# First-layer weights read with a step of two columns, second-layer weights two rows a partition

## The chip, the cores and the metric

The kernel runs on one core of one Trainium2 chip. Times are device microseconds of a whole execution. The time before is the median of three runs, 296.78 us (296.77 to 299.02). One execution was taken by the hardware profiler; its own time was 297.07 us, of which the profile shows a span of 295.2 us.

The engines are named as in the profile: PE is TensorE's matmul, PEld its weight load (which overlaps the matmul before it), DVE VectorE, ACT ScalarE, POOL GpSimd, SP SyncE. An engine with a q behind it is that engine's instruction queue.

## What is computed

A strided sparse attention on 8 batches of 8 heads, 576 positions and 64 features, and a two-layer network on its output. Four heads of each batch look at the last 32 positions, the other four at every 32nd position.

```python
scores = scale * np.matmul(q, k.transpose(0, 1, 3, 2))
mask_local = (rel >= 0) & (rel < stride)
mask_strided = (rel >= 0) & (pos[None, :] % stride == pos[:, None] % stride)
...
attn_out = np.matmul(attn, v)
x = attn_out.transpose(0, 2, 1, 3).reshape(B * S, H * D)     # 4608 x 512
h = x @ w_in                                                 # w_in 512 x 2048
r = np.maximum(h, 0.0)
out = (r * r) @ w_out                                        # w_out 2048 x 512
```

## The kernel before

The attention's output is kept transposed in four tiles `xt[0]` to `xt[3]` of 128 features by 4,608 tokens, in bf16. The network runs over nine chunks of 512 tokens. In each chunk the first layer has 16 *groups*, one for each block `ff` of 128 hidden features: four matmuls (`mm1`, L748) over the four chunks `kk` of the 512 features, with 128x128 weights out of `w_in_b` and 512 tokens of `xt[kk]` as the moving operand, summed in one PSUM bank. ACT takes the bank through Relu (L754), DVE squares the result into `g_sb` (L758). The second layer then has 16 groups of four matmuls (`mm2`, L854) with `g_sb` as weights and 512 columns of `w_out_b` as the moving operand; ACT copies the sum out (L858) and SP stores it. The last two chunks do the second layer with seven products instead of eight (L824), in a 4-byte type.

The order of all work is written by hand. `BATCH0` is a list of steps for the first batch's attention, and in it stand the first matmuls of the network: `P0.01` runs `mm1` of kk = 0 for ff = 0 and 1, `P2.012` kk = 2 for ff = 0, 1 and 2, and so on, in the order 0, 2, 1, 3 of kk, as the four `xt` become ready. Between them stand `E1a/6` (unit 1's transposes, L729, and ACT's copy into `xt[1]`, L732) and `O3/2` (unit 3's 16 small matmuls, L674, and DVE's product into `xt[3]`, L676). The number behind a slash is the PSUM bank. `NP` is the number of groups opened in this way; group `NP` takes the first bank of the pool `pt`, the later ones those of `ph` in turn. After `BATCH0` comes a numbered list of groups, and `PLAN` says which attention steps and loads stand ahead of which group.

The weights are loaded by POOL's DMA queue, which also changes their type from 4 bytes to bf16. `w_in_b` is a tile [128, 4, 2048]: partition, kk, column. It is loaded in four pieces (`load_w_in`, L462) while the attention starts: piece 1 is kk = 0 and 2, piece 2 is kk = 1 and 3, each for the first columns; pieces 3 and 4 are all kk for two later ranges of columns. `w_out_b` is [128, 16, 512]; it is loaded in four pieces of four chunks (`load_w_out`, L466), after the scratch data of the first batch that lie in it (q's and k's rows, and bias terms) have been used.

Waits are set by the recording layer: it compares what an instruction reads with what earlier instructions write, and puts a wait for the writer's semaphore on the reader. Each matmul has a weight load as an instruction of its own ahead of it, with waits of its own. PE runs its matmuls in the order of the program.

Of the kernel before, what the change touches and what calls it, by code (L numbers as in the profile page):

```python
# [13 lines left out]


FIRST = (0, 2, 1, 3)
NP = 5
BATCH0 = """
    c0qa c0kv T0qa/6 w1/7 T0kv/4 z w1/7 S0/0,2 W0q0v/4 W0q1v/5 b2.0/0 W0k0v/6 W0k1a/7 b2.1/2 b3.0/4 S2
    c1qv c1kv T1qv/6 T1kv/7 S3.0 b3.1/0 S3.1 b1.0/2 S1.0 b1.1/6 S1.1 H0v D0/4 N2/0 D1/6 E0a/4 N3/2 O2/0  # L20
    P0.01 E1a/6 P0.2/7 P2.012 O3/2 P0.34/0,1 P2.34 P1.01234 P3.0 P3.1 P3.2 P3.3 P3.4
"""
PLAN = """
0: l1q4+5 l1k4+5
# [143 lines left out]
def kernel(  # L168
# [9 lines left out]
    nc = tc.nc  # L178
# [45 lines left out]
    def bank(nm):  # L224
        if places:
            return all_banks[places.pop(0)]
        t = banks[nm].pop(0)
        banks[nm].append(t)
        while id(t) in unread:
            run_due(lambda x: x[1] == unread[id(t)])  # L230
        return t
# [27 lines left out]
    w_in_b = singles.tile([128, 4, d_ff], BF16)  # L259
    w_out_b = singles.tile([128, 16, d_model], BF16)  # L260
# [8 lines left out]
    rv0 = b0[:, n_s:n_s + 8 * S].bitcast(FP32).rearrange("p (u c) -> p u c", u=4)  # L269

    w_in_v = moe_w_in.rearrange("(c p) f -> p c f", p=128)
    w_out_v = moe_w_out.rearrange("(c p) f -> p c f", p=128)

    units = [(b, p) for b in range(B) for p in range(H // 2)]
    st = {}
# [181 lines left out]
            st.setdefault(4 * b + u, {})["v"] = t[:, u]  # L457

    def load_w_in(i):
        f = slice(*((0, 640), (0, 640), (640, 1344), (1344, 2048))[i])  # L460
        c = (slice(0, 4, 2), slice(1, 4, 2), slice(0, 4), slice(0, 4))[i]
        nc.gpsimd.dma_start(out=w_in_b[:, c, f], in_=w_in_v[:, c, f])  # L462

    def load_w_out(i):
        c = slice(4 * i, 4 * (i + 1))
        nc.gpsimd.dma_start(out=w_out_b[:, c, :], in_=w_out_v[:, c, :])  # L466

    clock = [0]
    pending = []
# [1 line left out]
    def later(n, fn, key=None):  # L471
        pending.append((clock[0] + n, key, fn))
# [267 lines left out]
    def mm1(c, ff, kks=range(4), order=range(4), pool=None):  # L740
        if c not in gs:
            gs[c] = g_pool.tile([128, 16, 512], BF16, name="g_sb")
        g = gs[c]
        if kks[0] == order[0]:
            phs[ff] = bank(pool or "ph")
        ph = phs[ff]
        for kk in kks:
            nc.tensor.matmul(ph, w_in_b[:, kk, 128 * ff:128 * (ff + 1)],  # L748
                             xt[kk][:, 512 * c:512 * (c + 1)],
                             start=(kk == order[0]), stop=(kk == order[-1]))  # L750
        if kks[-1] != order[-1]:
            return
        r = r_pool.tile([128, 512], BF16, name="r")
        nc.scalar.activation(r, ph, AF.Relu)  # L754
        if c in SEVEN:
            later(1, lambda: squares(c, ff, r))
            return
        later(1, lambda: nc.vector.tensor_tensor(g[:, ff, :], r, r, op=ALU.mult))  # L758
# [22 lines left out]
    def squares(c, ff, r):  # L781
        g, i = gs[c], ff % 8
        if not ss:
            att.close()
            late = ctx.enter_context(tc.tile_pool(name="sums", bufs=1, reuse_waits="tile"))
            for nm in ("1", "2", "3", "4", "a"):
                ss[nm] = late.tile([128, 8, 2, 128], mybir.dt.float32r, name=f"s{nm}")
        nc.vector.tensor_tensor(g[:, ff, :], r, r, op=ALU.mult)  # L788
        if ff < 8:
            return  # L790
        S = {k: x[:, i] for k, x in ss.items()}
        a1, a2 = (g[:, k, :].rearrange("p (u t c) -> p u t c", u=2, t=2) for k in (i, ff))
        nc.gpsimd.tensor_copy(S["a"], a2[:, :, 1])  # L793
        nc.vector.tensor_tensor(S["1"], a1[:, :, 1], a2[:, :, 1], op=ALU.add)
        nc.vector.tensor_tensor(S["2"], S["1"], a1[:, :, 0], op=ALU.subtract)
        last = lambda: nc.vector.tensor_tensor(S["4"], a2[:, :, 0], S["2"], op=ALU.subtract)
        later(15 + (4, 4, 5, 6, 7, 8, 9, 10)[i] - 2 * i, last)
        if i < 7:
            return
        for k in range(0, 8, 4):  # L800
            a1 = g[:, k:k + 4, :].rearrange("p k (u t c) -> p (k u) t c", u=2, t=2)
            nc.vector.tensor_tensor(ss["3"][:, k:k + 4].rearrange("p k u c -> p (k u) c"), a1[:, :, 0], a1[:, :, 1],
                                    op=ALU.subtract)
# [71 lines left out]
    def first_part(kks, ffs):  # L875
        for ff in ffs:
            mm1(0, ff, kks, FIRST, None if ff < 2 else "py")

    def run_step(word):
# [40 lines left out]
        elif op == "C":  # L920
            load_str_tall(int(arg[:-1]), arg[-1])
        elif op == "Q":
            load_qk_rows(int(arg[:-1]), arg[-1])
        elif op == "X":
            transpose_str(int(arg[:-1]), arg[-1])
        elif op == "A":
            transpose_cast(int(arg[:-1]), arg[-1])
        elif op == "R":
            order_local(int(arg[:-2]), arg[-2], ENG[arg[-1]])
        elif op == "Y":  # L930
            transpose_local(int(arg))
        elif op == "V":
            (load_v_local_sw if int(arg) > 2 else load_v_local_all)(int(arg))
        elif op == "U":
            load_v_str(int(arg))
        elif op == "B":
            spread_v_str(int(arg[0]), int(arg[1]), ENG[arg[2]])
        elif op == "l":
            load_qk_local_sw(int(arg[0]), [int(x) for x in arg[2:].split("+")], arg[1])
        elif op == "r":  # L940
            load_str_rows(int(arg[0]), arg[1])
        elif op == "i":
            load_w_in(int(arg))
        elif op == "o":
            load_w_out(int(arg))
        elif op == "z":
            late_constants()
        else:
            raise ValueError(word)
# [64 lines left out]
    for i in range(4):  # L1014
        load_w_in(i)
# [8 lines left out]
    def add(c, kind, i, pool=None):  # L1024
        if kind == 0:
            groups.append(lambda: None)
        elif kind == 1:
            groups.append(lambda: mm1(c, i, pool=pool))
        elif c in SEVEN:
            groups.append(lambda: mm2_7(c, i) if i < 14 else None)  # L1030
        else:
            groups.append(lambda: mm2(c, i, pool))

    for ff in range(16):
        add(0, 1, ff, {NP: "pt", 8: "py"}.get(ff)) if ff >= NP else add(0, 0, ff)
    for part in range(4):
# [58 lines left out]
```

## Time and profile before

| | |
|---|---|
| median of three runs | 296.78 us |
| the profiled execution | 297.07 us |
| its span | 295.2 us |
| matmuls of the first layer (L748), in the records | 557, 131.7 us busy |
| matmuls of the second layer (L854), in the records | 432, 100.9 us busy |
| first and last start of a first-layer matmul | 17.2 and 278.2 us |
| issue of w_in's four pieces by POOL | from 7.6 to 9.8 us |
| issue of w_out's four pieces by POOL | 15.3 to 32.6 us |

Lines of a timeline give the start, the duration from the first start to the last end, the engine, the line, the operation and the count; in brackets stands the idle time before it and what ended it. A matmul's duration in the records is modelled and longer than the distance to the next one, since matmuls are pipelined; the distance between starts is what counts. Some records of matmuls are missing. In rows of one line of code, durations stand as smallest, median and largest.

### The profile page before, as it was taken

The numbers are of one execution on the slowest core, as the hardware profiler recorded it, in microseconds if no ns is written. First come the engines' busy times: TensorE is split into PE (matmuls) and PEld (weight loads), VectorE is DVE, ScalarE is ACT, GpSimd is POOL, SyncE is SP. The second block draws the span as 40 slices with busy tenths as digits, with TensorE's granted clock in tenths as the row PEclk, the third lists the DMA queues.
The fourth block names the chain that finished last, engine by engine and source line by source line (L and its number), as shares of the span: only waits on it lengthen the run. The fifth ranks groups of instructions, "written<-read, shape, count | busy, mean of one in ns | idle before, by whom it ended". The sixth has DMA issues, their size and how long they took to land.

```text
span 295.2 us, 5895 instructions
## 1 busy us (share of the span) xinstructions
PE 286.3 (97%) x2177; PEld 155.7 (53%) x2212; DVE 210.5 (71%) x553; ACT 170.7 (58%) x321; POOL 83.0 (28%) x123
## 2 busy tenths in 40 slices
PE   7899999999999999999999999999999999999995
PEld 3554555545545454554454445544454444894594
DVE  6557687697666759678367835675489969968983
ACT  3758846775668736774577447645665466307610
POOL 8874743004513008119303800000000013102300
PEclk9999999999999999999999999999999999999999
DMA  7999999999999999999999999411011110021003
GB/s 149 188 207 204 192 198 190 150 204 215 147 138 213 117 163 201 136 166 141 216 159 147 165 186 147 83 56 73 36 23 52 58 54 0 1 104 42 0 2 142
DMA packets 91724, 37.38 MB, mean 127 GB/s; under 512 B 77548, under 2 KB 85830, under 8 KB 91696
## 3 DMA queue, kind: packets, MB, share of 16 engines
q0 software_dynamic: 50608, 18.33, 57.2%
q1 hardware_dynamic: 40944, 18.62, 34.3%
q8 instruction: 17, 0.28, 0.4%
q14 instruction: 11, 0.09, 0.1%
q10 hardware_dynamic: 144, 0.07, 0.1%
HBM read 37.22 MB, written 9.44 MB: 158 GB/s over the span
## 4 chain that ended last, share of the span: by engine, by line
PE 94%; DMA 2%; issue 1%; DVE 1%; ACT 0%; POOL 0%; DVEq 0%; POOLq 0%
PE psb L748 42%; PE psb L854 33%; PE psb L824 9%; DMA w_out_b<-in_k_dram 2%; PE psb L707 2%; PE psb L625 1%; PE psb L611 1%; PE psb L622 1%; PE psb L587 1%; PE psb L542 1%; PE psb L490 1%; PE psb L729 0%; PE psb L512 0%; PE psb L337 0%; DVE x_l L696 0%
## 5 line engine op out<-in xcount | busy, mean ns | idle before, releaser
L748 PE MATMUL psb<-xt,w_in_b 128*128 128x512 bf16 x557 | 131.7, 379 | 1.1
L754 ACT ACTIVATE r<-psb 128x512 bf16<-128x512 f32 x144 | 85.4, 599 | 47.2 <-PE psb L748 41.8
L854 PE MATMUL psb<-w_out_b,g_sb 128*128 128x512 bf16 x432 | 100.9, 379 | 1.1 <-issue 0.5
L748 PEld LDWEIGHTS <-w_in_b 128*128 128x128 bf16 x576 | 53.2, 97 | 58.3 <-issue 0.9
L758 DVE TENSOR_TENSOR g_sb<-r 128x512 bf16<-128x512 bf16 x112 | 47.1, 423 | 37.0 <-ACT r L754 36.1
L854 PEld LDWEIGHTS <-g_sb 128*128 128x128 bf16 x448 | 41.0, 97 | 44.7
L793 POOL CAST sa<-g_sb 128x256 fp32r<-128x256 bf16 x16 | 9.7, 607 | 100.3 <-DVE g_sb L788 100.3
L638 DVE TENSOR_TENSOR xt<-psb,rv 64x144 bf16<-64x144 f32 x84 | 26.2, 311 | 11.5 <-ACT rv L630 10.4
L858 ACT COPY y<-psb 128x512 f32<-128x512 f32 x28 | 16.6, 592 | 29.4 <-PE psb L854 28.4
L628 ACT ACTIVATE rv<-psb 128x432 f32<-128x432 f32 (+1 forms) x21 | 10.5, 501 | 12.8 <-PE psb L622 12.8
L713 DVE TENSOR_TENSOR x_l<-psb,rinv 96x384 bf16<-96x384 f32 x28 | 15.5, 553 | 1.0
L365 POOL DMA_DIRECT2D q_t<-in_q_dram x6 | 3.4, 569 | 45.3 <-DMA qT_s<-q_t 44.0
L788 DVE TENSOR_TENSOR g_sb<-r 128x512 bf16<-128x512 bf16 x32 | 13.0, 420 | 3.7 <-ACT r L754 3.7
L598 ACT ACTIVATE e<-psb 128x384 bf16<-128x384 f32 x30 | 12.0, 510 | 4.2 <-PE psb L587 4.2
L594 DVE TENSOR_TENSOR e<-e,mask_all 128x576 bf16<-128x576 bf16 x20 | 8.4, 456 | 7.3 <-ACT e L598 7.2
L294 POOL DMA_DIRECT2D k_l<-in_k_dram x16 | 12.2, 765 | 3.6 <-DMA v_st<-in_v_dram 3.6
L612 ACT ACTIVATE e<-psb 128x432 bf16<-128x432 f32 (+1 forms) x21 | 10.4, 496 | 4.0 <-PE psb L611 4.0
L645 DVE TENSOR_TENSOR xt<-psb,rv 64x270 bf16<-64x270 f32 (+1 forms) x28 | 9.8, 425 | 3.7 <-ACT rv L630 3.5
L824 PE MATMUL psb<-t,s 128*128 128x256 f32 x96 | 12.2, 283 | 0.0
L294 POOL DMA_DIRECT2D q_l<-in_q_dram x16 | 11.6, 728 | 0.7 <-DMA k_l<-in_k_dram 0.7
L824 PEld LDWEIGHTS psb<-t,s 128*128 128x128 f32 x96 | 11.6, 189 | 0.0
L630 ACT ACTIVATE rv<-rv 128x432 f32<-128x432 f32 (+1 forms) x21 | 11.2, 532 | 0.7
(135 smaller groups left out, 311.0 us busy)
## 6 DMA issues: line engine op xcount, KB each, us to landing
out_dram<-y SPq DMA_DIRECT2D x35, 256.0 KB, 3.8
w_out_b<-in_moe_w_out_dram POOLq DMA_DIRECT2D x4, 512.0 KB, 15.3
q_t<-in_q_dram POOLq DMA_DIRECT2D x7, 288.0 KB, 7.2
k_t<-in_k_dram POOLq DMA_DIRECT2D x7, 288.0 KB, 6.8
vl<-in_v_dram POOLq DMA_DIRECT2D x6, 288.0 KB, 7.3
v_st<-in_v_dram POOLq DMA_DIRECT2D x7, 216.0 KB, 7.8
w_in_b<-in_moe_w_in_dram POOLq DMA_DIRECT2D x2, 704.0 KB, 13.8
k_l<-in_k_dram POOLq DMA_DIRECT2D x16, 72.0 KB, 7.8
```

The lines of the kernel that those rows point to most:

```text
L294: nc.gpsimd.dma_start(out=t[:, :, hh, :], in_=src[b, 2 * p + hh].rearrange("(t p) d -> p t d", p=QL))
L598: nc.scalar.activation(e[:, row, 4 * QL * i:4 * QL * (i + 1)], bk[row][i][:, 0:4 * QL], AF.Exp, scale=scale)
L630: nc.scalar.activation(rv, rv, AF.Exp, scale=-1.0)
L638: nc.vector.tensor_tensor(to[:, :, NJ * part:NJ * (part + 1), par], of, by, op=ALU.mult)
L713: nc.vector.tensor_tensor(x, po[0:QL, :, 0:D], rinv[0:QL].to_broadcast([QL, NL, D]), op=ALU.mult)
L748: nc.tensor.matmul(ph, w_in_b[:, kk, 128 * ff:128 * (ff + 1)], xt[kk][:, 512 * c:512 * (c + 1)], start=(kk == order[0]), stop=(kk == order ...
L754: nc.scalar.activation(r, ph, AF.Relu)
L758: later(1, lambda: nc.vector.tensor_tensor(g[:, ff, :], r, r, op=ALU.mult))
L788: nc.vector.tensor_tensor(g[:, ff, :], r, r, op=ALU.mult)
L824: nc.tensor.matmul(pa, a, b, start=k == 0 and n not in "273", stop=k == 7, skip_group_check=True)
L854: nc.tensor.matmul(py, g[:, ff, 128 * j:128 * (j + 1)], w_out_b[:, ff, :], start=(ff == 0), stop=(ff == 15))
L858: nc.scalar.copy(y, py)
```

## The change

`w_out`'s rows are laid two to a partition: chunks 2m and 2m + 1 of `w_out_b` hold, on partition p, the rows 256m + 2p and 256m + 2p + 1, so a DMA's run in memory is two rows long. The hidden features of two neighbouring groups are interleaved to fit: group ff takes every second column out of the 256 columns of its pair. The first two pieces of `w_in` hold 512 columns instead of 640, the other two 768 instead of 704. Four groups instead of five are opened in `BATCH0`.

```diff
-NP = 5
+NP = 4
 BATCH0 = """
 ...
-    P0.01 E1a/6 P0.2/7 P2.012 O3/2 P0.34/0,1 P2.34 P1.01234 P3.0 P3.1 P3.2 P3.3 P3.4
+    P0.01 E1a/6 P0.2/7 P2.012 O3/2 P0.3/0 P2.3 P1.0123 P3.0 P3.1 P3.2 P3.3
 """
...
-    w_out_v = moe_w_out.rearrange("(c p) f -> p c f", p=128)
+    w_out_v = moe_w_out.rearrange("(m p c) f -> p m (c f)", p=128, c=2)
...
     def load_w_in(i):
-        f = slice(*((0, 640), (0, 640), (640, 1344), (1344, 2048))[i])
+        f = slice(*((0, 512), (0, 512), (512, 1280), (1280, 2048))[i])
         c = (slice(0, 4, 2), slice(1, 4, 2), slice(0, 4), slice(0, 4))[i]
         nc.gpsimd.dma_start(out=w_in_b[:, c, f], in_=w_in_v[:, c, f])

     def load_w_out(i):
         c = slice(4 * i, 4 * (i + 1))
-        nc.gpsimd.dma_start(out=w_out_b[:, c, :], in_=w_out_v[:, c, :])
+        nc.gpsimd.dma_start(out=w_out_b[:, c, :].rearrange("p (m c) f -> p m (c f)", c=2),
+                            in_=w_out_v[:, 2 * i:2 * i + 2])
...
         for kk in kks:
-            nc.tensor.matmul(ph, w_in_b[:, kk, 128 * ff:128 * (ff + 1)],
+            nc.tensor.matmul(ph, w_in_b[:, kk, 256 * (ff // 2):256 * (ff // 2 + 1)].rearrange("p (f c) -> p c f", c=2)[:, ff % 2],
                              xt[kk][:, 512 * c:512 * (c + 1)],
                              start=(kk == order[0]), stop=(kk == order[-1]))
```

## The prediction

> **What bounds the kernel now.** I read the page first: busy shares, then the chain that ended last.
>
> ```profile
> span 295.2 us, 5895 instructions
> PE 286.3 (97%) x2177; PEld 155.7 (53%) x2212; DVE 210.5 (71%) x553; ACT 170.7 (58%) x321; POOL 83.0 (28%) x123
> PE 94%; DMA 2%; issue 1%; DVE 1%; ACT 0%; POOL 0%; DVEq 0%; POOLq 0%
> ```
>
> PE is the bound: 286.3 of 295.2 us busy, and 94% of the chain. An edit can therefore gain only where PE waits, and loses wherever it makes PE wait. The view of waits for PE over the first 60 us says what it waits for, and the windows say how little of that is left later:
>
> ```profile
> engine line waited for: us in total, times, longest us
> PE psb L871 <- DVE xt L980: 1.3, 1, 1.3
> PE psb L347 <- DMA w_out_b<-in_k_dram: 0.8, 1, 0.8
> PE psb L729 <- DVE x_l L696: 0.5, 1, 0.5
> PE psb L542 <- DVE kTl L497: 0.4, 1, 0.4
> ```
> ```profile
> 18.10:25.00 6.90, 6.85 (x46) 3.14 (x46) 3.26 (x7) 4.25 (x9) 3.03 (x4) 1.00 1.21 208
> 34.00:200.00 166.00, 164.39 (x1259) 82.96 (x1281) 115.22 (x319) 103.08 (x199) 47.77 (x66) 1.00 1.31 161
> ```
>
> (Columns: length, then busy time of PE, PEld, DVE, ACT, POOL, the clock, the DMA share, GB/s.) No wait for a load of w_in or of w_out by moe_w_out is on the list; the one w_out_b row is k's rows, parked in that tile. From 18.10 to 25.00 PE is busy 6.85 of 6.90 us: there is no slack in which a new wait could hide.
>
> **A new wait: all of w_in before the second chunk of it.** In the built program's order of PE's instructions, three waits have moved. Before, the weight loads wait for piece 1 at P0's first matmul, piece 2 at P1's first, piece 3 at the sixth group's, piece 4 at the eleventh's. After, P0's first still waits for piece 1 alone, but the first weight load of P2 (kk = 2, ff = 0) waits for pieces 2, 3 and 4 together. The data need none of it: P2 reads chunk 2, columns 0 to 511, which is in piece 1. My reading is that a weight slice with a step of two is compared with the written blocks by its first and last element, so that chunk 2 counts as overlapped by each piece that begins in an earlier chunk and ends in a later one; chunk 0's first columns lie ahead of the others. When is PE there, and when does the last piece land?
>
> ```profile
> 17.58 0.42 PE L729 MATMUL psb<-ident,x_l 96*128 96x96 bf16 x6
> 17.84 1.03 PE L748 MATMUL psb<-xt,w_in_b 128*128 128x512 bf16 x4
> 18.80 0.45 PE L674 MATMUL psb<-e,g_sb 72*64 72x72 bf16 x16
> 19.18 9.24 PE L748 MATMUL psb<-xt,w_in_b 128*128 128x512 bf16 x41
> ```
> ```profile
> L462 POOL DMA_DIRECT2D w_in_b<-in_moe_w_in_dram x4: 738/742/785, 7.6 to 9.8; - x4
> DMA to landing us min/median/max: 8.8/11.0/15.2
> ```
> ```profile
> 25.27 0.54 POOL L427 DMA_DIRECT2D v_st<-in_v_dram  x1 [2.57 <-DMA w_in_b<-in_moe_w_in_dram]
> ```
> ```profile
> 2.76 6.77 DMA w_out_b<-in_k_dram
> 9.52 0.05 issue
> 9.57 0.70 PE psb L347 x12
> ```
>
> The row at 17.84 is P0.2 and P2's three matmuls. A matmul of 512 columns is shown with 0.379 us but they follow each other by (1.03 - 0.38) / 3 = 0.217 us, so PE comes to P2 at 17.84 + 0.22 = 18.06. The last piece is issued at 9.8 and the longest landing is 15.2 us: 25.0, which POOL's row confirms (its v_st load, free to go at 22.70, was held by a w_in landing until 25.27). From a landing to the matmul that waited for it the chain shows 0.05 us (9.52 to 9.57). PE would go on at 25.05: **7.0 us** of idle. Behind the waiting load in PE's order stand P2, unit 3's 16 small matmuls (L674) and all later work; DVE's xt of unit 3, ACT's and DVE's evictions wait for those. Nothing of this can move up, since matmuls run in program order.
>
> The loads themselves hardly move that landing: the four pieces hold the same 4.19 MB as before, on the same queue, behind the same loads, with 1,536 pieces of row in both versions (rows of 2 KB and 3 KB instead of 2.5 and 2.75). Pieces 2 to 4 land within 25.0 - 16.4 = 8.6 us; I take 0 and keep 0.5 us either way. POOL, the issuing engine, isn't held by the wait: what it issues next waits for landings and for PE work that lies before P2; the first of its loads that waits for later PE work is
>
> ```profile
> 36.60 0.54 POOL L365 DMA_DIRECT2D q_t<-in_q_dram  x1 [1.34 <-PE psb L542]
> ```
>
> and moves with PE.
>
> **The clock after that idle time.** Only the start of this kernel shows PE after a long rest.
>
> ```profile
> 1.26 4.02 PE L871 MATMUL psb<-xt 128*128 128x512 bf16 x9 [1.26 <-DVE xt L980]
> 5.53 0.38 PE L871 MATMUL psb<-xt 128*128 128x512 bf16 x1
> L871 PE MATMUL psb<-xt x11: 381/634/634, 1.3 to 6.0; 128*128 128x512 bf16 x11
> ```
>
> The same 128x512 matmul takes 634 ns there and 381 ns from 5.53 on, and the first nine follow each other by (4.02 - 0.63) / 8 = 0.42 us instead of 0.217: half rate for 5.53 - 1.26 = 4.3 us. Half of that, **2.1 us**, is lost if 7.0 us of idle put PE back to that state. No row of before shows an idle time between 1.3 us and that, so the bounds are 0 and, if the slow stretch is half as long again, 3.2 us; I take 2.1, from the only row in which PE starts from rest. The Trainium skill ("TensorE: Matmul & The Clock Gate", section "HAM oscillation — how this bites in real kernels") says that an idle gap of more than about 3.4 us throttles the clock again; by it the 7.0 us are enough and the sum is the one below, without it 2.1 us less; the rule speaks against this change, and no row of before can test it.
>
> **The weight loads with a step of two.** 576 of them.
>
> ```profile
> L748 PEld LDWEIGHTS <-w_in_b 128*128 128x128 bf16 x576 | 53.2, 97 | 58.3 <-issue 0.9
> L824 PEld LDWEIGHTS psb<-t,s 128*128 128x128 f32 x96 | 11.6, 189 | 0.0
> 278.40 3.82 PE L824 MATMUL psb<-w_out_b,g_sb 128*128 128x256 bf16 x32
> 281.98 4.03 PE L824 MATMUL psb<-t,s 128*128 128x256 f32 x32
> 285.85 2.06 PE L824 MATMUL psb<-t,sa 128*128 128x256 f32 x16
> 38.67 0.20 PE psb L611 x8
> ```
>
> No bf16 load of before has a step; the nearest row is the load of 4-byte elements, whose reads are as far apart: 189 ns against 97. Even so it lies under matmuls that last 217 ns, and the 32 such matmuls from 281.98 to 285.85 come every 121 ns, against 112 in the bf16 rows before: so a load can be followed by the next within 121 ns. Inside a run of L748 that is hidden. It would show only where a run begins behind short matmuls (L611: 0.20 / 8 = 25 ns each); by the program's order that is 44 places, such as
>
> ```profile
> 219.11 0.34 PE L707 MATMUL psb<-vl,e 128*128 128x65 bf16 x6
> 219.29 3.62 PE L748 MATMUL psb<-xt,w_in_b 128*128 128x512 bf16 x15
> ```
>
> so at most 44 x (121 - 25) ns = 4.2 us, and 0 if the step costs nothing. A gain is excluded: the reads are no shorter. I take 0, since the type and the count of elements are those of the 97 ns row, and keep 4.2. By the Trainium skill (same page, section "Weight-path perf modes — Fast Weight Load (FWL) and DoubleRow") the fast load holds for 128 weights that aren't fp32 at any column step from -1,023 to 1,024 elements; by that rule the term is 0, by the 189 ns row up to 4.2; no load here has a step, so the trace doesn't say.
>
> **Four groups instead of five.** The fifth group's four matmuls (0.87 us) move from the first part to just behind it: same work on PE. What it thins is a cover. DVE's xt of unit 3 is needed by P3:
>
> ```profile
> 19.36 0.76 DVE L676 TENSOR_TENSOR xt<-psb,g_sb 128x576 bf16<-128x576 f32 x1 [1.44 <-PE psb L674]
> 21.55 4.05 ACT L754 ACTIVATE r<-psb 128x512 bf16<-128x512 f32 x8 [2.65 <-PE psb L748]
> ```
>
> DVE's row ends at 20.12, 1.32 us after L674 began (18.80). Nine matmuls lay between, now six: 0.38 + 6 x 0.217 = 1.68 us, still more than 1.32. Without that cover it would cost up to 0.94 us; at half rate it only grows. Group 5 takes the first bank of the other pool, empty since unit 1's copy; ACT needs 4.05 / 8 = 0.5 us per eviction against 0.87 us per group. Cost 0.
>
> **w_out in rows of two.** Half as many, longer rows. PE waits for none of these loads now, and after a stall of PE they have 9 us more: 0.
>
> **Sum.** The profiled execution took 297.07 us (span 295.2 and 1.87 around it): + 7.0 + 2.1 + 0 + 0 = 306.2. It lies 0.29 above the median of 296.78, so **305.9 us**.
>
> **The rivals.**
> - *The idle time doesn't slow the clock.* For it: PEclk is full in all 40 slices of the page, the start too, so that row can't show it; against it the 634 ns. 305.9 - 2.1 = 303.8. Chance 0.08.
> - *Stall and slow clock, and the stepped loads show at the 44 places.* For it: the 189 ns; against: two bytes each, as before. 305.9 to 310.1; at 121 ns each, 310.1. Chance 0.10.
> - *Not slower: the new wait finds its pieces landed.* If w_in's four pieces went fast enough that the fourth is there when PE comes to P2, PE doesn't stop, the clock stays, and the time is 296.8. The point is 18.06 us; by 21 the loss would fall under 1%. The first piece is there by 7.6 + 8.8 = 16.4, so three pieces would have to follow within 1.7 us instead of 8.6. Against it stand all rows of landings. Chance 0.03, for a mistake of mine in what the wait covers.
>
> **How the numbers follow.** The likeliest case has what is left, 0.79; its own range is 304.6 to 307.5 (landing 0.5 us either way, slow stretch by 1.1 either way, not both in full). The range 303.8 to 308.0 adds the first rival and the lower half of the second; left out are the third and the rest of the second, 0.03 + 0.05, and some 0.1 for a slow stretch or a landing beyond the bounds. 1%, 3.0 us, is about what a measurement of this kernel tells from no change (its runs go from 296.77 to 299.02). All cases but the third lie above that: slower 0.95, within 1% 0.04 (the third, and a landing some microseconds earlier), faster 0.01.
>
> **What would show it.** PE idle for about 7 us from 18 us on, ended by the landing of w_in_b; in the page's slices PE falls in the third and fourth. The first L748 matmuls behind it at over 600 ns, for some 4 us. PEld of L748 tells of the step: 97 ns as before, or near 189, and the starts of L748 behind L707 and L611 whether it shows. ACT's first evictions move from 21.55 to about 30. I am wrong if PE runs on at 18.06, if it goes on much before 25, if its first matmuls last 380 ns, or if L748's runs cost more than 217 ns a matmul.

## The result, and the profile after

The changed kernel takes 306.06 us (median of four runs, 304.91 to 307.35) against 296.77 us before. The ratio of the means of all runs is 1.030, with a 95% interval of 1.023 to 1.036. The forecast was 305.9. The profiled execution is the shortest of the four, 304.91 us with a span of 303.1 us; it is 7.8 us above the profiled execution of before, and 1.2 us below its own median, which matters below.

The two pages first, before and after: PE busy and the clock in 40 slices (7.4 and 7.6 us long), then, of the changed kernel, the chain by engine and by line.

```profile
PE   7899999999999999999999999999999999999995
PEclk9999999999999999999999999999999999999999
```
```profile
span 303.1 us, 5931 instructions
PE   8927999999999999999999999999999999999995
PEclk9986999999999999999999999999999999999999
PE 91%; DMA 4%; POOL 2%; issue 2%; DVE 0%; DVEq 0%; POOLq 0%
PE psb L749 42%; PE psb L855 32%; PE psb L825 9%; DMA w_in_b<-in_moe_w_in_dram 4%; PE psb L708 2%; PE psb L626 1%; PE psb L612 1%; PE psb L623 1%; PE psb L588 1%; PE psb L491 1%; PE psb L543 1%; POOL w_in_b L462 0%; POOL xt L306 0%; POOL vl L440 0%; PE psb L337 0%
```

Before, PE is at 9 tenths in every slice from the third to the last but one. Now the third is at 2 and the fourth at 7, and the clock falls to 8 and 6 tenths in the same two. DMA's share of the chain has risen from 2 to 4%, and the loads on it are new: w_in's, where before's chain has k's rows.

The timeline of PE around that place (start, first start to last end, engine, line, operation, count):

```profile
17.11 0.42 PE L730 MATMUL psb<-ident,x_l 96*128 96x96 bf16 x6
17.37 0.38 PE L749 MATMUL psb<-xt,w_in_b 128*128 128x512 bf16 x1
24.30 1.44 PE L749 MATMUL psb<-xt,w_in_b 128*128 128x512 bf16 x3 [6.55 <-issue]
25.67 0.69 PE L675 MATMUL psb<-e,g_sb 72*64 72x72 bf16 x16
26.29 9.97 PE L749 MATMUL psb<-xt,w_in_b 128*128 128x512 bf16 x42
```

P0.2 runs alone at 17.37. P2's three matmuls, which followed it at once before, start at 24.30. PE would have come to them at 17.37 + 0.22 = 17.59, so the stop costs 6.7 us. That it is a wait although the view says "issue" is seen from who waited for w_in's loads, and from the event that PE's weight-load queue held (L749 is the changed kernel's mm1):

```profile
who waited for it (us, times):
  PEld L749: 6.8, 1
  PE psb L749: 6.6, 1
  POOL v_st L427: 2.8, 1
...
DMA to landing us min/median/max: 8.0/10.0/14.6
```
```profile
L749 PE MATMUL psb<-xt,w_in_b x576: 376/379/634, 16.7 to 286.0; 128*128 128x512 bf16 x192
L749 PEldq EVENT_SEMAPHORE  x2: 51/3764/7477, 16.8 to 121.1; - x2
```

The queue began to wait at 16.8 and was released 7.48 us later, at 24.28. The last piece was issued at 9.6 and landed 14.6 us later, at 24.2. The matmuls behind it last up to 634 ns, the value that only the start of the kernel showed before. The windows (length, busy time of PE, PEld, DVE, ACT, POOL, clock, DMA share, GB/s) show when:

```profile
17.60:20.90 3.30, 0.15 (x1) 0.00 (x0) 0.00 (x0) 0.82 (x2) 2.22 (x3) 1.00 1.16 209
20.90:24.30 3.40, 0.00 (x0) 0.03 (x1) 0.00 (x0) 0.00 (x0) 0.70 (x1) 0.50 1.20 205
24.30:27.70 3.40, 3.40 (x23) 1.38 (x24) 0.76 (x1) 0.00 (x0) 1.95 (x6) 0.50 1.23 212
27.70:34.00 6.30, 6.30 (x31) 2.80 (x29) 3.41 (x8) 4.53 (x9) 5.19 (x8) 1.00 1.56 190
```

The clock is full for 3.3 us of the stop, then half until 27.7. PE works 3.4 us of that, and loses half, 1.7 us. The sum is 6.7 + 1.7 = 8.4; PE reached this place 0.5 us earlier than in the execution of before (P0.2 at 17.37 instead of 17.84), and 8.4 - 0.5 = 7.9 is the difference of the two spans.

Behind it nothing is lost. From the first second-layer matmul to the end of the last row of PE, before and after:

```profile
33.87 0.38 PE L854 MATMUL psb<-w_out_b,g_sb 128*128 128x512 bf16 x1
...
289.63 2.06 PE L824 MATMUL psb<-tb,s 128*128 128x256 f32 x16
```
```profile
41.72 1.03 PE L855 MATMUL psb<-w_out_b,g_sb 128*128 128x512 bf16 x4
...
297.46 2.05 PE L825 MATMUL psb<-tb,s 128*128 128x256 f32 x16
```

291.69 - 33.87 = 257.82 us before, 299.51 - 41.72 = 257.79 after. Most of the 576 first-layer weight loads lie in that stretch, all with a step of two.

### The profile page after: what moved, and what is told of

Its sections match the earlier page's. It is cut to its first block, busy times and chain, and to the rows that moved or that the text cites. A ratio compares the mean times of both kernels' runs of the same rounds, so it can differ in the third digit from the quotient of the medians.

```text
span 303.1 us, 5931 instructions
## 1 busy us (share of the span) xinstructions
PE 290.9 (96%) x2212; PEld 156.6 (52%) x2212; DVE 211.4 (70%) x553; ACT 170.9 (56%) x321; POOL 81.9 (27%) x123
## 4 chain that ended last, share of the span: by engine, by line
PE 91%; DMA 4%; POOL 2%; issue 2%; DVE 0%; DVEq 0%; POOLq 0%
PE psb L749 42%; PE psb L855 32%; PE psb L825 9%; DMA w_in_b<-in_moe_w_in_dram 4%; PE psb L708 2%; PE psb L626 1%; PE psb L612 1%; PE psb L623 1%; PE psb L588 1%; PE psb L491 1%; PE psb L543 1%; POOL w_in_b L462 0%; POOL xt L306 0%; POOL vl L440 0%; PE psb L337 0%
## 5 line engine op out<-in xcount | busy, mean ns | idle before, releaser
L749 PE MATMUL psb<-xt,w_in_b 128*128 128x512 bf16 x576 | 134.7, 381 | 6.7 <-issue 6.6
L755 ACT ACTIVATE r<-psb 128x512 bf16<-128x512 f32 x144 | 85.5, 598 | 55.3 <-PE psb L749 51.4
L855 PE MATMUL psb<-w_out_b,g_sb 128*128 128x512 bf16 x448 | 103.2, 379 | 0.0
L749 PEld LDWEIGHTS <-w_in_b 128*128 128x128 bf16 x576 | 53.5, 98 | 65.7 <-issue 9.0
L639 DVE TENSOR_TENSOR xt<-psb,rv 64x144 bf16<-64x144 f32 x84 | 26.2, 312 | 11.5 <-ACT rv L631 10.4
L825 PEld LDWEIGHTS psb<-t,s 128*128 128x128 f32 x96 | 11.6, 188 | 0.0
```

Of the source, the lines that this page charges most:

```text
L639: nc.vector.tensor_tensor(to[:, :, NJ * part:NJ * (part + 1), par], of, by, op=ALU.mult)
L749: nc.tensor.matmul(ph, w_in_b[:, kk, 256 * (ff // 2):256 * (ff // 2 + 1)].rearrange("p (f c) -> p c f", c=2)[:, ff % 2], xt[kk][:, 512 * c ...
L825: nc.tensor.matmul(pa, a, b, start=k == 0 and n not in "273", stop=k == 7, skip_group_check=True)
L855: nc.tensor.matmul(py, g[:, ff, 128 * j:128 * (j + 1)], w_out_b[:, ff, :], start=(ff == 0), stop=(ff == 15))
```

## The experiments

The theory: PE waits for w_in's last piece because a stepped read is compared with the loads by its first and last element, and after that rest it runs at half clock for some microseconds; step, rows and groups cost nothing by themselves. The rivals: the stepped weight loads cost time; the groups, the pieces or w_out's rows do. `mm1` has another line number in some of the variants (L748 to L755); its tile in the rows shows it.

**Each piece in a tile of its own** (`e1_own_tiles`).

```diff
-    w_in_b = singles.tile([128, 4, d_ff], BF16)
+    w_in_p = [singles.tile([128, n, w], BF16, name=f"w_in{i}") for i, (n, w) in enumerate(((2, 512), (2, 512), (4, 768), (4, 768)))]
...
-        nc.gpsimd.dma_start(out=w_in_b[:, c, f], in_=w_in_v[:, c, f])
+        nc.gpsimd.dma_start(out=w_in_p[i], in_=w_in_v[:, c, f])
+
+    def w_in_of(kk, m):
+        if m < 2:
+            return w_in_p[kk % 2][:, kk // 2, 256 * m:256 * m + 256]
+        return w_in_p[2 + m // 5][:, kk, 256 * ((m - 2) % 3):256 * ((m - 2) % 3) + 256]
...
```

> The changed kernel with each of w_in's four pieces in a tile of its own; the step of two, w_out's rows and the four opened groups stay. P2 then waits for piece 1 alone, which it has. If the joint wait and the clock behind it are all of the loss (my theory), PE runs on at 18 us, no matmul of the first layer after the start takes 634 ns, and the time is 296.8 within 0.6 us. If the stepped weight loads cost something, PE still doesn't stop at 18 us, but the time stays above: up to 301 us if each of the 44 places behind short matmuls shows 96 ns.

297.33 us (median of 12 runs) against 297.16 for the kernel before in the same runs: ratio 1.001, 0.997 to 1.005. PE runs on:

```profile
17.56 1.03 PE L754 MATMUL psb<-xt,w_in 128*128 128x512 bf16 x4
18.52 0.45 PE L680 MATMUL psb<-e,g_sb 72*64 72x72 bf16 x16
18.90 2.33 PE L754 MATMUL psb<-xt,w_in 128*128 128x512 bf16 x10
21.48 7.08 PE L754 MATMUL psb<-xt,w_in 128*128 128x512 bf16 x32 [0.26 <-DMA w_in<-in_moe_w_in_dram]
```

The whole loss is gone with the wait, and the step, the rows and the four groups are all still there. The last row holds something that my prediction didn't have: with four groups opened, the fifth needs piece 3 four matmuls earlier, and in this execution PE waited 0.26 us for it. The ten matmuls ahead of it take 2.33 us, 9 x 0.217 + 0.38, so P3 doesn't wait for unit 3's xt.

**No step** (`e4_no_step`): weights read as before, w_out's rows and their loads as before (those lines are left out here), the rest as changed.

```diff
...
-            nc.tensor.matmul(ph, w_in_b[:, kk, 256 * (ff // 2):256 * (ff // 2 + 1)].rearrange("p (f c) -> p c f", c=2)[:, ff % 2],
+            nc.tensor.matmul(ph, w_in_b[:, kk, 128 * ff:128 * (ff + 1)],
...
```

> The changed kernel with weights read without a step and w_out's rows laid as before; the pieces of 512 and 768 columns and the four opened groups stay. If the step is what brings the joint wait, P2 waits for piece 1 alone and the time is 296.8 within 0.6 us. If the pieces' sizes or the four groups cost anything, it is above that: up to 0.9 us for xt of unit 3 coming late, or the wait for piece 3 at the fifth group, which is now needed 0.9 us earlier.

297.23 us against 297.16, ratio 1.002 (0.999 to 1.004). P2's matmuls follow P0.2 in one row:

```profile
17.82 1.03 PE L748 MATMUL psb<-xt,w_in_b 128*128 128x512 bf16 x4
```

PE has no wait for w_in; its weight load has one of 0.4 us, which is not among PE's waits. Without the step the joint wait is gone (w_out's rows, put back with it, are tested by themselves next); pieces and groups are worth nothing that these runs can tell.

**w_out's rows alone** (`e5_w_out_alone`): the kernel before with these lines of the change. It leaves out the regrouping of w_in's columns to match, so it computes another output, with the same loads and the same work.

```diff
-    w_out_v = moe_w_out.rearrange("(c p) f -> p c f", p=128)
+    w_out_v = moe_w_out.rearrange("(m p c) f -> p m (c f)", p=128, c=2)
...
-        nc.gpsimd.dma_start(out=w_out_b[:, c, :], in_=w_out_v[:, c, :])
+        nc.gpsimd.dma_start(out=w_out_b[:, c, :].rearrange("p (m c) f -> p m (c f)", c=2),
+                            in_=w_out_v[:, 2 * i:2 * i + 2])
```

> The kernel before with w_out loaded in rows of two a partition and nothing else changed; w_in's columns are not regrouped to match, so hidden features meet the wrong rows of w_out and the output differs from the reference's. My theory: PE waits for none of these loads, so 296.8 within 0.6 us, although the loads have half the rows. If w_out's rows matter for PE in some way that the wait list doesn't show, the time leaves that band on either side.

297.23 us against 297.07, ratio 1.001 (0.998 to 1.004).

**The same tile, laid out by piece** (`e6_by_piece`): tests how the wait is found. One tile as in the changed kernel, but the pieces lie one behind the other in it, and piece 1's two chunks are neighbours.

```diff
-    w_in_b = singles.tile([128, 4, d_ff], BF16)
+    w_in_b = singles.tile([128, 4 * d_ff], BF16)
...
-        nc.gpsimd.dma_start(out=w_in_b[:, c, f], in_=w_in_v[:, c, f])
+        o, n = ((0, 2), (1024, 2), (2048, 4), (5120, 4))[i]
+        t = w_in_b[:, o:o + n * (f.stop - f.start)].rearrange("p (c f) -> p c f", c=n)
+        nc.gpsimd.dma_start(out=t, in_=w_in_v[:, c, f])
...
```

> The changed kernel with one tile for w_in as in it, but laid out inside in the order of the pieces (piece 1, 2, 3, 4 one behind the other), so that no piece's first and last element enclose another's. Steps, w_out and groups stay. If a stepped read is compared by its first and last element, P2 waits for piece 1 alone and the time is 297 within 0.6 us, as with four tiles. If any stepped read of a tile waits for all of the tile's loads, P2 stops as in the changed kernel: 306.

297.26 us against 297.07, ratio 1.001 (0.997 to 1.005); P2 follows P0.2 at once:

```profile
17.93 1.03 PE L755 MATMUL psb<-xt,w_in_b 128*128 128x512 bf16 x4
```

So neither one tile nor the step by itself brings the wait: it takes the step together with pieces that lie between one another's first and last element. The runs show which reads wait; how the recording layer compares them is inferred from that. (Its profiled execution took 300.1 us, with one wait of 1.8 us for a transposing load at 90 us that the median doesn't have.)

**Only the last piece apart** (`e2_last_apart`): a shorter stop.

```diff
-    w_in_b = singles.tile([128, 4, d_ff], BF16)
+    w_in_b = singles.tile([128, 4, 1280], BF16)
+    w_in_c = singles.tile([128, 4, 768], BF16, name="w_in_c")
...
-        nc.gpsimd.dma_start(out=w_in_b[:, c, f], in_=w_in_v[:, c, f])
+        nc.gpsimd.dma_start(out=w_in_c if i == 3 else w_in_b[:, c, f], in_=w_in_v[:, c, f])
...
```

> The changed kernel with only piece 4 of w_in in a tile of its own. P2 waits for pieces 2 and 3. The landing theory: PE stops from 17.6 until piece 3 has landed (20.4 in the changed kernel's trace), 2.9 us, which is less than the 3.1 us of rest after which the clock fell there; the clock stays full, so 296.8 + 2.9 = 299.7 us. If the clock falls for any stop of this kind, 1.7 us or more on top, 301.4. If the loss comes from the weight loads and not from the wait's length, about 306 as in the changed kernel.

303.69 us (median), four runs from 301.82 to 303.80; ratio 1.020 (1.017 to 1.024). That is above the 299.7 and the 301.4 that I had set down. The profiled one is that of 301.82:

```profile
17.42 0.38 PE L753 MATMUL psb<-xt,w_in_b 128*128 128x512 bf16 x1
20.52 1.14 PE L753 MATMUL psb<-xt,w_in_b 128*128 128x512 bf16 x3 [2.71 <-DMA w_in_b<-in_moe_w_in_dram]
```
```profile
17.60:20.50 2.90, 0.20 (x1) 0.00 (x0) 0.00 (x0) 0.88 (x2) 2.55 (x3) 1.00 1.15 208
20.50:20.90 0.40, 0.38 (x2) 0.21 (x3) 0.00 (x0) 0.00 (x0) 0.00 (x0) 0.97 1.22 223
20.90:24.30 3.40, 3.40 (x24) 1.28 (x22) 0.76 (x1) 0.00 (x0) 0.70 (x1) 0.50 1.20 205
24.30:34.00 9.70, 9.70 (x56) 4.66 (x55) 6.03 (x15) 7.48 (x14) 6.56 (x12) 1.00 1.43 198
```

The stop is 2.9 us as expected and ends with piece 3, so its length is set by the landing. My expectation for the clock was wrong: it fell, and it fell 0.4 us after PE had gone on, at 20.9. It then stayed at half for 3.4 us of full work: 2.9 + 1.7 = 4.6, against 301.82 - 297.16 = 4.7. The other three runs are 1.9 us longer, and no trace of them was kept. A second slow stretch of that length would cost 1.7. The mean granted clock is on record for each run: 0.994 for the profiled one, which is its 3.4 us at half clock, and 0.989 and 0.987 for two of the others, which is about 7 to 8 us and fits a second stretch. The third has 0.994 too, at 303.80 us, so its extra time stays open.

**A stop filled with work** (`e3_busy_wait`): the wait stays, PE doesn't rest.

```diff
-    P0.01 E1a/6 P0.2/7 P2.012 O3/2 P0.3/0 P2.3 P1.0123 P3.0 P3.1 P3.2 P3.3
+    P0.01 E1a/6 P0.2/7 w31/1 P2.012 O3/2 P0.3/0 P2.3 P1.0123 P3.0 P3.1 P3.2 P3.3
```

> The changed kernel with 31 matmuls of 128x512 on a tile of zeros, whose sums nothing reads, put between P0.2 and P2; they fill the stop (31 x 0.217 = 6.7 us). The joint wait stays. If the clock behind the stop is part of the loss, it stays full now and the time falls by 1.7 us or more against the changed kernel, to 303.3 to 304.4 us, with the first matmuls of P2 at 379 ns. If the loss behind the stop has another cause (evictions, banks, the weight loads), the time stays at 306.

304.32 us (median), four runs from 303.85 to 304.71; ratio 1.024 (1.021 to 1.027).

```profile
17.88 6.85 PE L872 MATMUL psb<-xt 128*128 128x512 bf16 x31
24.74 0.81 PE L749 MATMUL psb<-xt,w_in_b 128*128 128x512 bf16 x3
```
```profile
24.70:34.00 9.30, 9.29 (x58) 4.26 (x58) 4.65 (x10) 5.37 (x10) 6.84 (x12) 1.00 1.44 198
```

P2's three matmuls now take 0.81 us instead of 1.44, the clock is full, and 1.7 us of the loss is gone (2.1 when each kernel is set against the kernel before of its own runs: 9.3 and 7.2 us), while PE comes to P2 later than in the changed kernel's trace (24.74 against 24.30). The clock is a part of the loss of its own. The mean granted clock of every run bears that out: 0.981 or 0.989 in all five executions of the changed kernel, 0.997 or more in all four with the stop filled, and 0.998 or more in 38 of the 42 of the kernel before that ran beside the experiments e1 to e7.

**The changed kernel once more** (`after_again`), for the spread of its times.

> The changed kernel once more, for its clock. In its first trace the clock was halved from 20.9 to 27.7, of which PE worked 3.4 us, and that execution was the shortest of four (304.91 against 305.78 to 307.35). If the slow stretch behind the stop differs from execution to execution, this one's time minus 304.91 is half of its slow working stretch minus 1.7, within 0.5 us. If something else spreads the times, the slow stretch is 3.4 us again whatever the time.

305.39 us, 0.48 above the first trace. The clock:

```profile
21.60:24.40 2.80, 0.00 (x0) 0.00 (x0) 0.00 (x0) 0.00 (x0) 0.27 (x1) 0.51 1.22 205
24.40:28.50 4.10, 4.05 (x24) 1.56 (x25) 0.76 (x1) 0.00 (x0) 2.28 (x7) 0.50 1.22 208
28.50:34.00 5.50, 5.45 (x26) 2.47 (x26) 3.04 (x8) 4.24 (x8) 4.58 (x5) 1.00 1.59 189
```

PE worked 4.05 us at half clock, which makes 2.0 - 1.7 = 0.3 us more than in the first trace; the rest is a stop that begins and ends 0.1 us later. The slow working stretch does differ from execution to execution.

**Larger steps** (`e8_step4`, `e9_step8`, `e7_step16`): the stepped loads by themselves. Each regroups w_in's columns and w_out's rows to match, here for 16:

```diff
-            nc.tensor.matmul(ph, w_in_b[:, kk, 256 * (ff // 2):256 * (ff // 2 + 1)].rearrange("p (f c) -> p c f", c=2)[:, ff % 2],
+            nc.tensor.matmul(ph, w_in_b[:, kk].rearrange("p (f c) -> p c f", c=16)[:, ff],
...
```

> The changed kernel with a step of 16 columns instead of two and w_out's rows 16 a partition. Each group now needs all columns, so already P0 has to wait for pieces 3 and 4: PE stops 0.9 us of work earlier than in the changed kernel, and at the same stretches of slow clock the time is 0.9 us above it, 307.0. If the weight loads slow with the step, the starts behind short matmuls spread (25 and 29 ns in the trace of before) and up to 4.2 us come on top, 311.

> The changed kernel with a step of four columns and w_out's rows four a partition, to see from which step the weight load slows: 98 ns at a step of two, 146 at 16, where some first-layer matmuls come later than 216 ns. If the load grows evenly with the step, about 105 ns here; if there is a threshold, 98. P2's joint wait stays, so PE stops until 24 to 25 us as in the changed kernel, and the time is within 2 us of 306.

> The same with a step of eight and w_out's rows eight a partition. P0 now needs piece 3 (20.4 us), and the group that opens the second half piece 4. Even growth: about 119 ns a load, and less than half of the 1.2 us that the step of 16 lost from its first second-layer matmul to the last of all. A threshold between eight and 16: 98 ns and none of that loss (257.5 us for that stretch).

308.74 us (median of four runs) for 16, which is neither the 307.0 nor the 311 that I had set down; 306.37 and 304.37 (one run each) for four and eight. These times hold stops and slow stretches of differing length, so the loads are read from their own rows; steps 2, 4, 8 and 16, one fence each (busy us, mean ns):

```profile
L749 PEld LDWEIGHTS <-w_in_b 128*128 128x128 bf16 x576 | 53.5, 98 | 65.7 <-issue 9.0
```
```profile
L748 PEld LDWEIGHTS <-w_in_b 128*128 128x128 bf16 x576 | 62.0, 114 | 59.1 <-issue 10.1
```
```profile
L748 PEld LDWEIGHTS <-w_in_b 128*128 128x128 bf16 x576 | 79.2, 146 | 41.8 <-DMA w_in_b<-in_moe_w_in_dram 4.8 <-issue 1.7
```
```profile
L748 PEld LDWEIGHTS <-w_in_b 128*128 128x128 bf16 x576 | 79.4, 146 | 42.8 <-issue 7.5
```

98, 114, 146 and 146 ns: neither of the two courses that I had set down, even growth or a threshold. The stretch from the first second-layer matmul to PE's last row is 257.8 us at a step of two, 258.0 at four, and 259.0 at eight and 16. The last of these from its rows, 303.03 - 44.01:

```profile
44.01 1.03 PE L854 MATMUL psb<-w_out_b,g_sb 128*128 128x512 bf16 x4
...
300.98 2.05 PE L824 MATMUL psb<-tb,s 128*128 128x256 f32 x16
```

So a large step does cost this kernel something, 1.2 us, but a step of two costs nothing. The stretch tells such differences: in the traces with a step of two of the changed kernel, once more, e1, e2 and e3 it goes from 257.79 to 257.81 us.

## Why the prediction was right

- **The new wait.** Forecast 7.0 us of stop from 18.06 to 25.05; measured 6.7, from 17.6 to 24.3. The place, what is waited for and the release by the fourth piece are as forecast. Both ends came earlier in this execution. The explanation by first and last element, an inference then, is borne out by the one tile laid out by piece. One reading beside it was wrong: the first of POOL's loads put down to PE work behind P2 isn't that at 36.60 but w_out's second, at 21.94 (first line). In the changed kernel it goes at 20.96 (second line), while PE stands still, so it didn't hang on that work and POOL wasn't held, as forecast. ACT's first eviction came at 28.7, not at about 30: with four groups, three matmuls fewer lie ahead of it, which the sign left out.

```profile
21.94 0.76 POOL L466 DMA_DIRECT2D w_out_b<-in_moe_w_out_dram  x1 [1.27 <-PE psb L748]
20.96 0.70 POOL L466 DMA_DIRECT2D w_out_b<-in_moe_w_out_dram  x1 [0.85 <-DMA w_in_b<-in_moe_w_in_dram]
```

- **The clock.** Forecast 2.1 us from the kernel's start, where PE runs at half rate for 4.3 us. Measured 1.7 and 2.0 us in two traces of the changed kernel; filling the stop takes 1.7 to 2.1 off the median. The Trainium skill's rule that speaks against the change ("TensorE: Matmul & The Clock Gate", "HAM oscillation — how this bites in real kernels": an idle gap of more than about 3.4 us throttles the clock) agrees with these traces, though a gap of 2.9 us did so too. That the clock would be halved behind the stop was right; that the size came near is partly luck, since the slow stretch doesn't start with PE's work, as it was priced, but within the stop, and its length differs. The three executions of the changed kernel that were not traced have a mean granted clock of 0.981 against 0.989, which is about 11.6 us at half clock instead of 6.7. That can cost up to 2.4 us more; they are 0.9 to 2.4 us longer than the profiled one, so longer slow stretches would account for the median's 1.2 us above it.
- **The weight loads.** Taken at 0, kept up to 4.2. Measured 0: 98 ns each, and 257.79 us against 257.82 for the rest of the kernel. The bound from the fp32 row was far too wide for a step of two. The place was well chosen: with steps of eight and 16 the loss does show behind short matmuls (last section).
- **Four groups.** Cost 0, as forecast, for the cover of unit 3's xt. The reasoning left out that the fifth group's piece 3 is needed earlier: 0.26 us in one trace, hidden in the changed kernel by the long stop.
- **w_out's rows.** 0, as forecast: no PE wait hung on them, and halving the rows left the time at a ratio of 1.001.
- **The sum.** 305.9 against 306.06. That it is so close is partly luck: in the profiled execution the stop was 0.3 us shorter than forecast, the clock's cost 0.4 less and the start 0.5 earlier, 1.2 us in all, and the median lies 1.2 us above that execution. In the ranges, 307.5 is both bounds in full (305.9 + 0.5 + 1.1), though the text says not both.

None of the variants beats the kernel before: with the wait away, the change is worth nothing either way, since PE waited neither for w_out's rows nor for w_in's first pieces.

## What to carry to other kernels

A change of an access pattern can change the waits, not only the access: before timing it, compare which loads the first readers wait for, and where the recording layer widens a read, lay the tile out so that no load's first and last element enclose another's. A stop of the engine that bounds the kernel costs more than its length when its clock falls with it, so price both, and the second as a range: in the two traces of the changed kernel it was 1.7 and 2.0 us. An engine that never waits for a load gains nothing from a faster load.

## What the runs showed of the hardware

The clock's fall isn't tied to the moment of the rest: in the kernel with the 2.9 us stop it fell 0.4 us after PE had gone on, for 3.4 us of full work. The slow stretches that the traces show are 3.4 us there (20.9 to 24.3) and 6.8 us in the changed kernel (20.9 to 27.7); with a step of four it was 10.2 us (19.5 to 29.7):

```profile
19.50:24.90 5.40, 0.04 (x1) 0.07 (x2) 0.00 (x0) 0.00 (x0) 1.63 (x2) 0.50 1.20 207
24.90:29.70 4.80, 4.80 (x26) 1.80 (x27) 0.76 (x1) 0.00 (x0) 2.79 (x8) 0.50 1.27 209
```

These are one, two and three times 3.4 us. The Trainium skill ("TensorE: Matmul & The Clock Gate", section "What's actually happening") has the clock set by windows of 3.4 us that run on whatever the kernel does; the traces agree. With a step of 16 the mean over the first 18 us is 0.82, or 6.5 us at half clock:

```profile
0.00:18.00 18.00, 15.40 (x165) 8.50 (x165) 9.81 (x34) 9.58 (x14) 15.99 (x27) 0.82 1.16 172
PE psb L347 <- DMA w_out_b<-in_k_dram: 0.9, 1, 0.9
```

So there the clock fell at about 11.5 us, some 7 us before PE's stop, and the longest wait of PE since its first matmul was one of 0.9 us (second line, out of the list of PE's waits; the row stands at 8.5 to 9.4). It stayed at half until 28.6, five times 3.4 us. A stop is not the only thing after which it falls, and what made it fall there was not settled. What a stop costs beyond its length therefore depends on where it falls among the windows, which differs from execution to execution.

A bf16 weight load of 128x128 takes 98 ns at a step of one and two columns, 114 at four and 146 at eight and 16. Though that is less than the 216 ns of the matmul above it, eight and 16 cost 1.2 us: the starts behind short matmuls stay at 25 and 29 ns at all steps, but in the stretch read above some 30 of the 451 first-layer starts that follow another in the records come 230 to 280 ns after it, not 216; with a step of two none does. At eight and at 16, all but one of these are the second matmul of a run that begins behind short ones (L490, L542, L611, L625, L707), the kind of place that the prediction had counted; 28 of them, about 36 ns late each, make 1.0 of the 1.2 us.
